# The head of a fused attention and feed-forward kernel: one written order, half of its early masks on VectorE, up weights in quarters

## The chip, the cores and the metric

The kernel runs on one core of one Trainium2 chip. The metric is device time in microseconds (us) of one execution; the median of the runs shown counts. A core has five engines that run their own instruction lists in order and meet at semaphores: TensorE (PE, with its weight loads PEld), VectorE (DVE), ScalarE (ACT), GpSimd (POOL) and SyncE (SP). POOL, SP and ACT also issue the transfers (DMAs).

## The reference

Causal attention over 8 sequences of 576 tokens with 8 heads of 64 columns and 16 extra "beacon" keys that no mask covers, and then a two-layer feed-forward with a leaky ReLU, in float32:

```python
k_all = np.concatenate([beacon_k, k], axis=2)
v_all = np.concatenate([beacon_v, v], axis=2)
scores = scale * np.matmul(q, k_all.transpose(0, 1, 3, 2))
causal[:, Nb:] = np.triu(np.ones((S, S), dtype=bool), k=1)
scores = np.where(causal, -1000000000.0, scores)
a = np.exp(scores - scores.max(-1, keepdims=True))
a /= a.sum(-1, keepdims=True) + 1e-09
x = np.matmul(a, v_all)            # then heads side by side: 4608 tokens x 512
h = x @ w_in                       # 512 x 2048
out = np.maximum(0.01 * h, h) @ w_out   # 2048 x 512
```

## The kernel before

**Units.** A unit g (0 to 31) is one pair of heads of one sequence; four units make a sequence. Keys of a unit lie in five blocks of up to 128 rows (the first holds the 16 beacons and 112 tokens). Scores are made transposed, keys on partitions and queries along the row, so a causal block needs work only on and above its diagonal.

**One unit's way.** Queries and keys are loaded as bf16 by POOL's DMAs (`load_qk`, L158) and turned by PE with an identity (`t_q`, L243), and DVE or ACT copy the result out of PSUM (L249). For unit 0 the keys come over SP in float32 (`first_k`), are cast by ACT and DVE (L928, L929) and turned at L238. `score` (L267) makes one of four groups n of score products in a PSUM tile, of which there are two, and ACT puts the exponential of it into `aT` (L276). The diagonal blocks then lose their lower triangle: `mask(g, part)` calls `triangle` (L289), a POOL affine select in place; part 0 is the first block, part 1 the blocks of groups 1 and 2, part 2 those of group 3. `value(g, half)` multiplies with the values (L359; half 0 is the first three query tiles, half 1 the last two), DVE takes the reciprocal of the row sums (L388) and multiplies (L389), and `finish` turns the result into `xT` (L405, copy at L410). Values of a sequence are loaded in five blocks (L209 the beacons, L214).

**The feed-forward.** An up step (`up`, L442) makes 128 of the 2048 hidden columns for 512 tokens in a PSUM bank, and ACT writes the leaky ReLU to `gT` (L450). A down step (`down`) multiplies `gT` with `w_out`: for the first 512 tokens four products of 512 columns each (L519), four steps making one tile of 128 tokens, and later in a scheme with seven products instead of eight (L544). `w_in` comes in two halves of 1024 columns (L131) and `w_out` in two (L137). DVE makes differences of `w_out` for that scheme (L468 to L472).

**The head and the rest.** The first two sequences (units 0 to 7) are the head; its order on every engine is the order in which the code is written, since the scheduler is told to keep it: some calls and strings that `run` reads step by step. From unit 8 on, the order follows from a list of events with due times, and there the scores are made in stretches of 512 columns (`stretch`, L314, exponentials L329 and L333) over queries and keys that DMA transposes lay out (`load_natural` L171, `turn_pair` L179). Head and rest meet in order too: the rest starts after the last step of the head. Small products with a tile of zeros (`unused`, L825; `unused_ahead`, L837) fill PE's early waits.

**The letters of `run`.** `l` load_qk, `q` and `k` turn queries or keys, `s` score, `m` mask, `v` value, `x` finish, `V` load of a value block, `u` up, `d` down, `i` and `o` loads of `w_in` and `w_out`, `N` load_natural, `T` turn_pair, `y` the transfer that turns unit 4's result, `b` the beacon columns of a later unit's keys, `t` the differences of `w_out`, `w` and `W` the products with zeros. After the letter stands the unit, then a group, half or engine: `s2.1` is group 1 of unit 2, and 1 as an engine is ACT.

**Queues.** PSUM has two score tiles and four banks that all else shares. POOL's DMAs use eight semaphores in turn: an issue waits until the transfer eight issues earlier has landed, and holds all that stands behind it on POOL, the selects too.

Of the kernel before, what the change touches and what calls it, by code (L numbers as in the profile page):

```python
# [9 lines left out]
BF16 = mybir.dt.bfloat16  # L10
AF = mybir.ActivationFunctionType
ALU = mybir.AluOpType
# [3 lines left out]
def kernel(  # L16
# [24 lines left out]
    RI = 9  # L41
# [47 lines left out]
    blank = singles.tile([128, 128], BF16, name="blank")  # L89
    w_in_sb = [singles.tile([128, NJ, DF // 2], BF16, name=f"w_in_sb{i}") for i in range(2)]  # L90
# [71 lines left out]

    def load_first_keys():
        for h in range(2):
            nc.sync.dma_start(out=first_k[h], in_=k[0, h].rearrange("(p i) d -> p i d", i=RI))
# [674 lines left out]

    NG = B * NPAIR
# [18 lines left out]
    def run(steps):  # L860
        for step in steps.split():
# [33 lines left out]
            elif op == "i":  # L895
                load_w_in(a[0])
            elif op == "o":
                load_w_out(a[0])
            elif op == "t":
                weight_sums(a[0])  # L900
            else:
                raise ValueError(step)
# [11 lines left out]
    with order:  # L914
        load_first_keys()
        load_beacon_k(0, 2, nc.scalar)
        nc.vector.memset(blank, 0.0)
        nc.vector.memset(ident, 0.0)
        run("l0.0 l1.0")
        make_identity(nc, ident, nomemset=True)  # L920
        make_ones()
        run("l1.1 l2.0 l2.1 V0.0 V0.1 l3.0 l3.1 V0.2 V0.3 V0.4 l4.0 l4.1 i0")
        make_pads()
        unused(13, 256)
        cast_beacon_k(0, 2, nc.scalar.copy)
        beacon_transposes(0, 2)
        unused(13)
        nc.scalar.copy(out=k_nat0[:, :, 0], in_=first_k[0])  # L928
        nc.vector.tensor_copy(out=k_nat0[:, :, 1], in_=first_k[1])  # L929
        run("q0.1 k0 w2.384 s0.0 m0.0 w3.256 s0.1 q1 s0.2 m0.1 k1 s0.3 m0.2")  # L930
        run("w2.384 s1.0 m1.0 q2 s1.1 k2 w2.384 s1.2 m1.1 w2.384 s1.3 m1.2 W0.0.4 s2.0 m2.0 W0.0.4 s2.1 W0.0.6 q3 l5.0 l5.1 s2.2 k3 w4.384 v0.0 m2.1 s2.3 i1 m2.2 W0.1.4 s3.0 m3.0 v1.0 s3.1 v0.1 s3.2 v1.1 m3.1 l6.0 l6.1 s3.3 x0.1 m3.2")
# [110 lines left out]
```

## Time and profile before

| | |
|---|---|
| runs | 325.3, 324.43, 329.58 us; median 325.3 us |
| profiled execution | span 323.8 us from its first to its last instruction; of its own time the profile gives no more than this span |
| PE busy | 314.3 us (97%) |
| DVE, ACT, POOL busy | 168.0, 203.8, 184.3 us |
| granted TensorE clock, mean | 1.000 |
| transfers | 39.78 MB, mean 123 GB/s |

An engine's busy share counts its own instructions; on POOL it counts the issue of DMAs, not the transfers. A timeline row holds the start, the length, the engine, the line, what is written and read, the count of merged instructions, and in brackets the idle time of the engine ahead of it with what ended it. A DMA's row is its issue; its landing shows where somebody waits for it. The chain of waits follows the program back from its last instruction.

### The profile page before, as it was taken

The page shows a single profiled execution, that of the slowest core. Times are in us where ns is not written, and L with a number is a line of the kernel's source. Part 1 is how long each engine was busy: PE and PEld are TensorE (multiplying, and loading weights), DVE is VectorE, ACT ScalarE, POOL GpSimd, SP SyncE. Part 2 cuts the span into 40 slices and gives each one's busy share as a digit, 9 for nine tenths or more (in the row PEclk, how much of TensorE's full clock was granted, in tenths as well). Part 3 has the DMA queues.
Part 4 walks back from the last instruction along what each step waited for, and adds up shares of the span by engine and source line. Part 5 has one row for each costly group of instructions (what it writes and reads, how often), then busy time and mean ns, then how long its engine had stood idle before and what let it go on. Part 6 is the DMA issues. An engine that isn't in the chain of part 4 may idle for free.

```text
span 323.8 us, 8701 instructions
## 1 busy us (share of the span) xinstructions
PE 314.3 (97%) x3468; PEld 219.1 (68%) x3494; DVE 168.0 (52%) x341; ACT 203.8 (63%) x346; POOL 184.3 (57%) x354
## 2 busy tenths in 40 slices
PE   7999999999999999999999999999999999999995
PEld 4575555444588557855788888656875697688784
DVE  3464245508255244444443454525464689577954
ACT  4968962387855786478746874687458547455510
POOL 8895868999996787659875977666221000000000
PEclk9999999999999999999999999999999999999999
DMA  8999999999999999999999999999222100200123
GB/s 137 129 189 192 124 214 140 169 177 188 135 152 160 216 138 129 114 186 97 141 176 174 99 143 119 188 128 129 44 81 82 26 2 32 75 25 2 65 67 130
DMA packets 155256, 39.78 MB, mean 123 GB/s; under 512 B 142368, under 2 KB 152480, under 8 KB 155216
## 3 DMA queue, kind: packets, MB, share of 16 engines
q0 software_dynamic: 99824, 18.54, 91.1%
q1 hardware_dynamic: 55120, 20.62, 38.3%
q8 instruction: 27, 0.44, 0.6%
q14 instruction: 13, 0.11, 0.1%
q10 hardware_dynamic: 272, 0.07, 0.1%
HBM read 37.22 MB, written 9.44 MB: 144 GB/s over the span
## 4 chain that ended last, share of the span: by engine, by line
PE 72%; DMA 14%; POOL 9%; ACT 3%; issue 1%; DVE 0%; POOLq 0%; ACTq 0%; SPq 0%
PE acc L442 24%; PE acc L544 19%; PE sc L544 11%; PE av L359 6%; PE sc L314 5%; PE acc L663 5%; DMA w_out_sb<-in_moe_w_out_dram 4%; DMA gsum<-in_k_dram 4%; POOL aT L289 3%; DMA k_nat<-in_k_dram 3%; DMA v_aug<-in_v_dram 2%; ACT aT L333 2%; DMA kT<-k_nat 2%; POOL gsum L158 1%; POOL v_aug L214 1%
## 5 line engine op out<-in xcount | busy, mean ns | idle before, releaser
L442 PE MATMUL acc<-xT,w_in_sb 128*128 128x512 bf16 (+1 forms) x537 | 116.5, 354 | 1.5 <-ACT aT L329 0.3
L450 ACT ACTIVATE gT<-acc 128x512 bf16<-128x512 f32 x124 | 70.8, 623 | 33.1 <-PE acc L442 32.6
L289 POOL TENSOR_SCALAR_AFFINE_SELECT aT<-aT 128x256 bf16<-128x256 bf16 (+2 forms) x160 | 59.7, 403 | 51.4 <-ACT aT L329 31.5
L442 PEld LDWEIGHTS <-w_in_sb 128*128 128x128 bf16 x560 | 51.7, 98 | 43.9 <-issue 2.9
L544 PEld LDWEIGHTS <-gT 128*128 128x128 bf16 x512 | 48.7, 98 | 7.7 <-issue 1.8
L333 ACT ACTIVATE aT<-sc 128x1024 bf16<-128x1024 f32 (+3 forms) x64 | 51.7, 892 | 0.0
L329 ACT ACTIVATE aT<-sc 128x512 bf16<-128x512 f32 (+3 forms) x64 | 29.0, 520 | 27.8 <-PE sc L314 27.8
L388 DVE RECIPROCAL rec<-av 128x6 f32<-128x6 f32 (+1 forms) x64 | 12.0, 187 | 65.0 <-PE av L359 64.4
L359 PEld LDWEIGHTS <-aT 128*128 128x128 bf16 (+1 forms) x960 | 36.9, 98 | 9.2 <-issue 1.4
L544 PEld LDWEIGHTS <-gsum 128*128 128x128 bf16 x384 | 36.5, 98 | 6.5 <-issue 0.4
L359 PE MATMUL av<-v_aug,aT 128*128 128x65 bf16 (+1 forms) x960 | 39.8, 194 | 0.8 <-DMA v_aug<-in_v_dram 0.4
L214 POOL DMA_DIRECT2D v_aug<-in_v_dram x40 | 34.1, 856 | 4.2 <-DMA w_in_sb<-in_moe_w_in_dram 3.8
L171 POOL DMA_DIRECT2D k_nat<-in_k_dram x48 | 34.8, 730 | 0.9 <-DMA w_out_sb<-in_moe_w_out_dram 0.3
L171 POOL DMA_DIRECT2D q_nat<-in_q_dram x48 | 34.8, 729 | 0.6 <-issue 0.4
L389 DVE TENSOR_TENSOR x_nat<-av,rec 128x384 bf16<-128x384 f32 (+1 forms) x64 | 31.4, 491 | 2.2
L544 PE MATMUL acc<-w_out_sb,gT 128*128 128x256 bf16 x240 | 28.9, 273 | 0.4 <-ACT gT L450 0.4
L276 ACT ACTIVATE aT<-sc 128x1024 bf16<-128x1024 f32 (+3 forms) x32 | 26.0, 874 | 4.7 <-PE sc L267 2.5
L314 PE MATMUL sc<-qT,kT 64*128 64x80 bf16 (+22 forms) x384 | 22.2, 250 | 0.3
L314 PEld LDWEIGHTS <-kT 64*128 64x128 bf16 x384 | 12.8, 94 | 11.2 <-issue 7.6
L544 PE MATMUL acc<-w_sum,gsum 128*128 128x256 bf16 x160 | 20.1, 273 | 0.0
L575 ACT COPY p<-acc 128x512 f32<-128x512 f32 x15 | 9.1, 604 | 16.8 <-PE acc L544 16.8
L785 DVE TENSOR_TENSOR gsum<-gT 128x1024 bf16<-128x1024 bf16 x16 | 11.0, 688 | 15.7 <-ACT gT L450 15.7
(95 smaller groups left out, 339.0 us busy)
## 6 DMA issues: line engine op xcount, KB each, us to landing
out_dram<-p SPq DMA_DIRECT2D x26, 256.0 KB, 3.2
q_nat<-in_q_dram POOLq DMA_DIRECT2D x48, 72.0 KB, 5.5
k_nat<-in_k_dram POOLq DMA_DIRECT2D x48, 72.0 KB, 5.3
v_aug<-in_v_dram POOLq DMA_DIRECT2D x24, 128.0 KB, 6.5
w_in_sb<-in_moe_w_in_dram POOLq DMA_DIRECT2D x2, 1024.0 KB, 12.4
w_out_sb<-in_moe_w_out_dram POOLq DMA_DIRECT2D x2, 1024.0 KB, 12.1
out_dram<-u SPq DMA_DIRECT2D x8, 256.0 KB, 2.7
gsum<-in_q_dram POOLq DMA_DIRECT2D x8, 144.0 KB, 7.1
```

The costliest lines, as they stand in the source:

```text
L171: nc.gpsimd.dma_start(out=t[:, :, par], in_=(q, k)[which][b, 2 * hp + par].rearrange("(t p) d -> p t d", p=NR),)
L214: nc.gpsimd.dma_start(out=dst[lo : ROWS[c], c, :, 0:D], in_=v[b, :, OFF[c] : OFF[c] + n].rearrange("h p d -> p h d"),)
L276: nc.scalar.activation(out=aT[:, :, c0 : c0 + w], in_=sc[:, :, 0:w], func=AF.Exp, scale=0.125)
L289: nc.gpsimd.affine_select(out=view, in_=view, compare_op=ALU.is_ge, fill=0.0, base=128 - n if lo == 0 else 0, channel_multiplier=-1, patte ...
L314: nc.tensor.matmul(out=(sc[par] if apart else sc[:, par])[:, at : at + b - a], lhsT=kT[ps_, c * 128 : (c + 1) * 128], rhs=qT[ps_, q0 : q0 ...
L329: nc.scalar.activation(out=probs[g][:, par, lo:hi], in_=sc[par][:, at : at + hi - lo], func=AF.Exp, scale=0.125)
L333: nc.scalar.activation(out=probs[g][:, :, lo:hi], in_=sc[:, :, at : at + hi - lo], func=AF.Exp, scale=0.125)
L359: nc.tensor.matmul(out=avv[:, n, 0 : D + 1], lhsT=aT[0 : ROWS[c], par, a0 : a0 + 128], rhs=va[0 : ROWS[c], c, 2 * hp + par, :], start=(c = ...
L389: nc.vector.tensor_tensor(out=x_nat[:, t0:t1].rearrange("p t e d -> p (t e) d"), in0=avv[:, :, 0:D], in1=rec[:, n0:n1, None].to_broadcast( ...
L442: nc.tensor.matmul(out=acc[:, lo:hi], lhsT=w_in_cols(fc, j), rhs=xT[:, j, x0 : x0 + hi - lo], start=(j == 0), stop=(j == NJ - 1), skip_gro ...
L450: nc.scalar.activation(out=gT[i][:, fc, :], in_=acc, func=AF.Prelu, alpha=0.01)
L544: nc.tensor.matmul(out=acc[:, lo : lo + HD], lhsT=left(i, n, fc, tile), rhs=right(n, fc), start=(lo == 0 and fc == 0), stop=(fc == HF - 1) ...
```

## The change

Four things are done in the head, and nothing behind it.

- A tile `kept` of ones, with zeros below its diagonal, is made once (a memset on DVE, an affine select on POOL). `mask` with a third argument multiplies the diagonal block with `kept` on VectorE, instead of the affine select on POOL. 12 of the 24 mask groups of units 0 to 7, with 20 of their 40 blocks, take this way.
- `w_in` is loaded in four pieces of 512 columns rather than in two of 1024.
- The calls between the strings get letters of their own (`F` first keys, `K`, `C`, `B` the first beacons' load, cast and turning, `h` the casts of unit 0's keys, `Z`, `I`, `J`, `j`, `O`, `P` constants, `L`, `c`, `D` the later beacons), so that all of the head is one string, `HEAD`.
- `HEAD` puts the steps in another order. The counts of score, value, transposing, up and down steps and of the products with zeros are the same as before.

```diff
+    kept = singles.tile([128, 128], BF16, name="kept")
...
-    def load_w_in(i):
-        n = DF // 2
-        loaded["w_in", i] = nc.gpsimd.dma_start(
-            out=w_in_sb[i], in_=w_in_r[:, :, i * n : (i + 1) * n]
+    def load_w_in(i, part=None):
+        lo, hi = (0, DF // 2) if part is None else (part * (DF // 4), (part + 1) * (DF // 4))
+        nc.gpsimd.dma_start(
+            out=w_in_sb[i][:, :, lo:hi], in_=w_in_r[:, :, i * (DF // 2) + lo : i * (DF // 2) + hi]
         )
...
-    def mask(g, part):
+    def mask(g, part, dve=0):
         aT = probs[g]
         for lo, n, rows in MASKS[part]:
-            triangle(aT, lo, n, rows)
+            if dve:
+                view = aT[0:rows, :, lo : lo + n]
+                at = 128 - n if lo == 0 else 0
+                nc.vector.tensor_tensor(
+                    out=view,
+                    in0=view,
+                    in1=kept[0:rows, None, at : at + n].to_broadcast([rows, 2, n]),
+                    op=ALU.mult,
+                )
+            else:
+                triangle(aT, lo, n, rows)
+
+    def make_kept():
+        nc.gpsimd.affine_select(
+            out=kept,
+            in_=kept,
+            compare_op=ALU.is_ge,
+            fill=0.0,
+            base=0,
+            channel_multiplier=-1,
+            pattern=[[1, 128]],
+        )
...
+    HEAD = "l0.0 Z I w13.256 l1.0 l1.1 w13 J F1 O w2.384 l3.0 l2.1 w3.256 l2.0 W0.0.4 K l3.1 V0.0 V0.1 q0.0 V0.2 l4.0 l4.1 F0 V0.4 w2.384 V0.3 C w2.384 h0.1 h1.0 i0.1 W0.0.6 q1 B j W0.1.4 k0.1 w2.384 P l5.0 s0.0 k1 s0.2 s0.3 i0.0 s1.0 m0.0.1 s0.1 m0.1.1 k2.1 w4.384 s1.1 q2 s1.2 W0.0.4 q3.0 s2.0 v0.0 s2.2 m1.1.1 q4.1 k3.0 s1.3 m0.2.1 m1.0.0 m1.2.0 s2.1 v1.0 s3.0 l5.1 m2.1.1 k4.0 s3.1 m2.0.0 v1.1 v0.1 l6.0 s2.3 m2.2.1 l7.1 l6.1 m3.0.1 i1.0 s3.2 m3.1 v2.0 s3.3 m3.2 V1.0 V1.2 x1.0 x0.1 v2.1 v3.0 v3.1 x2.1 q5.0 s4.0 V1.1 k5.0 x3.0 q6.1 s4.1 s4.2 u i1.1 u V1.3 m4.0.1 s5.0 k7.1 s4.3 k6.0 u l7.0 u V1.4 o0 s5.2 u u L m4.1.1 m4.2.0 v4.0 s5.1 m5.0.1 u s6.0 o1 s5.3 m5.1.1 v5.0 m6.0.0 u u s6.2 s6.1 m5.2.0 u N8.0 N8.1 v4.1 q7.0 c u v5.1 u s7.0 x5.0 m6.1.1 u y4 T8 m7.0 u s7.1 d u s7.3 s6.3 d m6.2 N9.0 s7.2 m7.1 D v6.0 v6.1 u m7.2 b8.2 v7.0 N9.1 V2.0 d N10.0 T9 v7.1 b10.2 N10.1 d T10 x6.1 b9.2 t0 d b11.2 x7.0 V2.1 d"
...
+            elif op == "F":
+                nc.sync.dma_start(out=first_k[a[0]], in_=k[0, a[0]].rearrange("(p i) d -> p i d", i=RI))
+            elif op == "h":
+                (dve, act)[a[1]](out=k_nat0[:, :, a[0]], in_=first_k[a[0]])
...
-        load_first_keys()
...
-        run("q0.1 k0 w2.384 s0.0 m0.0 w3.256 s0.1 q1 s0.2 m0.1 k1 s0.3 m0.2")
...
+        run(HEAD)
```

What this makes of three places:

VectorE, around the copies of unit 0's keys, before (tp is a PSUM tile of turned columns, k_nat unit 0's cast keys, gsum the buffer of its raw ones):

```order
L121 MEMSET aT_92 128x2x24 x2
L121 MEMSET aT_93 128x2x24 x2
L201 COPY kT<-tp 64x8x16 x2
L929 CAST k_nat_97<-gsum_96 64x9x64
L249 COPY kT<-tp 128x117
L249 COPY kT<-tp 128x459
L249 COPY qT<-tp 128x576
```

and now, from the memset of the value buffers' ones on:

```order
L126 MEMSET v_aug_90 128x40
L246 COPY qT<-tp 128x576
L942 CAST k_nat_98<-gsum_97 64x9x64
L246 COPY qT<-tp 128x576
L198 COPY kT<-tp 64x8x16 x2
L246 COPY kT<-tp 128x459
```

The queries of units 0 and 1 are copied by DVE around the cast of unit 0's keys, where before ACT copied unit 0's queries and DVE unit 1's came later; the beacon columns come after them, and the first 117 key columns go to ACT.

VectorE, from the first reciprocal (half 0 of unit 0's values) on, now (aT_91 to aT_94 are the probabilities of units 0 to 3, rec and x_nat the normalised result of a half):

```order
L406 RECIPROCAL rec<-av 128x6
L407 TENSOR_TENSOR x_nat<-av,rec 128x384
L285 TENSOR_TENSOR aT_92<-aT_92,kept 128x2x128 x2
L246 COPY kT<-tp 128x576
L285 TENSOR_TENSOR aT_91<-aT_91,kept 128x2x128
L285 TENSOR_TENSOR aT_91<-aT_91,kept 80x2x80
L406 RECIPROCAL rec<-av 128x6
L407 TENSOR_TENSOR x_nat<-av,rec 128x384
L285 TENSOR_TENSOR aT_93<-aT_93,kept 128x2x128 x2
L246 COPY kT<-tp 128x576
```

where before the halves followed each other with nothing between but the copies:

```order
L388 RECIPROCAL rec<-av 128x6
L389 TENSOR_TENSOR x_nat<-av,rec 128x384
L388 RECIPROCAL rec<-av 128x6
L389 TENSOR_TENSOR x_nat<-av,rec 128x384
L388 RECIPROCAL rec<-av 128x4
L389 TENSOR_TENSOR x_nat<-av,rec 128x256
```

Nine products with `kept` and the copies of units 3 and 4's keys and of unit 5's queries and keys now stand between that first reciprocal and the copy of unit 3's result, ahead of which no up step can begin.

POOL, behind the second half of `w_out`, before (q_nat and k_nat are loads of units 8 to 10, bk the later beacons, v_aug sequence 2's values):

```order
L188 CAST bk<-bk_raw 128x384
L171 DMA q_nat<-in_q_dram 96x6x64 x2
L289 AFFINE_SELECT aT_93<-aT_93 128x2x112
L289 AFFINE_SELECT aT_93<-aT_93 128x2x128 x3
L289 AFFINE_SELECT aT_93<-aT_93 80x2x80
L171 DMA k_nat<-in_k_dram 96x6x64 x2
L229 COPY kT<-bkT 128x16 x4
L171 DMA q_nat<-in_q_dram 96x6x64 x2
L171 DMA k_nat<-in_k_dram 96x6x64 x2
L209 DMA v_aug_88<-in_beacon_v_dram 16x8x64
```

and now:

```order
L168 DMA q_nat<-in_q_dram 96x6x64 x2
L307 AFFINE_SELECT aT_94<-aT_94 128x2x128 x3
L307 AFFINE_SELECT aT_94<-aT_94 80x2x80
L226 COPY kT<-bkT 128x16
L168 DMA k_nat<-in_k_dram 96x6x64 x2
L206 DMA v_aug_89<-in_beacon_v_dram 16x8x64
L211 DMA v_aug_89<-in_v_dram 112x8x64
L168 DMA q_nat<-in_q_dram 96x6x64 x2
L226 COPY kT<-bkT 128x16
L168 DMA k_nat<-in_k_dram 96x6x64 x2
```

The first two value loads of sequence 2 now stand ahead of unit 10's queries and keys.

More of the change, by code (lines that the diff above doesn't have):

```diff
@@ L161, in load_qk @@
         )
-    def load_first_keys():
-        for h in range(2):
-            nc.sync.dma_start(out=first_k[h], in_=k[0, h].rearrange("(p i) d -> p i d", i=RI))
     def load_natural(g, which):
@@ L895, in run @@
             elif op == "i":
-                load_w_in(a[0])
+                load_w_in(*a)
             elif op == "o":
```

47 lines of the change are left out of this document (25 added, 22 removed).

## The prediction

> **What bounds the kernel now.** I read the page first, then the chain of waits, then the timeline of the first 80 us.
>
> ```profile
> PE 314.3 (97%) x3468; PEld 219.1 (68%) x3494; DVE 168.0 (52%) x341; ACT 203.8 (63%) x346; POOL 184.3 (57%) x354
> PE   7999999999999999999999999999999999999995
> DMA  8999999999999999999999999999222100200123
> ```
>
> PE is busy in 314.3 of 323.8 us, and in the first slices too. The change leaves the number and kinds of PE's instructions as they are, so all it can win is idle time of PE: 9.5 us in the whole span, some of it before the first transfer can land. The transfers are at 9 tenths from the second slice to two thirds of the span. The chain shows where they hold the head:
>
> ```profile
> 6.09 7.05 DMA v_aug<-in_v_dram
> 22.86 11.57 DMA gsum<-in_k_dram
> 39.96 13.69 DMA w_out_sb<-in_moe_w_out_dram
> 64.21 8.28 DMA k_nat<-in_k_dram
> 72.54 5.26 DMA kT<-k_nat
> 77.85 0.67 PE sc L314 x10
> ```
>
> A value load issued at 6.09 lands at 13.14, a key load of 22.86 at 34.43, the second half of `w_out` of 39.96 at 53.65: seven, twelve, fourteen us later, since each stands behind a queue of others. So the loads of the head are one long line that runs without a break, and the time of a landing is the sum of what stands ahead of it. At 77.80 the keys of unit 11 are laid out, and PE takes them 0.05 us later. PE and the loads arrive together there; a PE that came earlier would wait.
>
> The timeline shows the few places where PE itself waits for a load or a mask (start, length, engine, line, work, idle before it):
>
> ```profile
> 5.91 0.47 PE L243 MATMUL tp<-ident,gsum 64*64 64x64 bf16 x18 [0.83 <-DMA gsum<-in_q_dram]
> 16.67 0.72 PE L359 MATMUL av<-v_aug,aT 128*128 128x65 bf16 x12
> 18.18 0.54 PE L359 MATMUL av<-v_aug,aT 128*128 128x65 bf16 x12
> 19.89 0.35 PE L359 MATMUL av<-v_aug,aT 80*128 80x65 bf16 x6 [0.39 <-DMA v_aug<-in_v_dram]
> 40.04 0.68 PE L359 MATMUL av<-v_aug,aT 128*128 128x65 bf16 x15 [0.19 <-POOL aT L289]
> 47.30 1.04 PE L519 MATMUL acc<-w_out_sb,gT 128*128 128x512 bf16 x4 [0.48 <-DMA w_out_sb<-in_moe_w_out_dram]
> 53.70 3.61 PE L519 MATMUL acc<-w_out_sb,gT 128*128 128x512 bf16 x15
> 53.94 0.72 POOL L171 DMA_DIRECT2D k_nat<-in_k_dram  x1 [0.34 <-DMA w_out_sb<-in_moe_w_out_dram]
> ```
>
> The twelve value products at 16.67 take 0.18 us longer than the same twelve at 18.18: I read that as the third value block landing at about 17.1. The third down step, at 53.70, begins when the second half of `w_out` has landed.
>
> **The change part by part.** *The start.* Rows before:
>
> ```profile
> 6.42 0.64 ACT L249 COPY qT<-tp 128x576 bf16<-128x576 bf16 x1 [1.98 <-PE tp L243]
> 5.62 0.74 DVE L929 CAST k_nat<-gsum 64x576 bf16<-64x576 f32 x1 [0.87 <-DMA gsum<-in_k_dram]
> 4.29 0.46 DVE L201 COPY kT<-tp 64x128 bf16<-64x128 bf16 x2 [2.21 <-PE tp L194]
> 7.31 0.39 PE L267 MATMUL sc<-qT,kT 64*128 64x512 bf16 x2
> 7.74 8.89 ACT L276 ACTIVATE aT<-sc 128x1024 bf16<-128x1024 f32 x11 [0.68 <-PE sc L267]
> ```
>
> The first query load still lands at about 5.9, so DVE's first copy still begins at 6.42. Then stand, one after the other on DVE, a query copy (0.76, the row further down), a cast (0.74), a second query copy (0.76) and the beacon columns (0.46): 6.42 + 2.72 = 9.14. The first score group follows at 9.2 instead of 7.31, the first exponential at 9.6 instead of 7.74. In between PE does products with zeros and a transposing that it did later before, so PE loses nothing yet; ACT is 1.9 us late. Eight exponentials of 0.81 (8.89 over 11) and one copy of 0.64 bring ACT to about 16.7, when the first value half is due. It still waits for the third value block, which has the same ten loads ahead of it as before: 17.1.
>
> *DVE from there to the first up step.* The first up step needs the copy of unit 3's result, and the order on DVE puts the following between the first reciprocal (17.43 before, and now) and the end of that copy. Means by form (busy us, mean ns):
>
> ```profile
> L249 DVE COPY qT<-tp 128x576 bf16<-128x576 bf16 x7 | 5.3, 756 | 12.7 <-PE tp L243 12.7
> L389 DVE TENSOR_TENSOR x_nat<-av,rec 128x384 bf16<-128x384 f32 x32 | 17.8, 557 | 1.1
> L389 DVE TENSOR_TENSOR x_nat<-av,rec 128x256 bf16<-128x256 f32 x32 | 13.6, 424 | 1.1
> L388 DVE RECIPROCAL rec<-av 128x6 f32<-128x6 f32 x32 | 6.2, 194 | 35.8 <-PE av L359 35.5
> L388 DVE RECIPROCAL rec<-av 128x4 f32<-128x4 f32 x32 | 5.8, 180 | 29.2 <-PE av L359 28.9
> L410 DVE COPY xT<-tp 128x576 bf16<-128x576 bf16 x6 | 2.7, 455 | 5.2 <-PE tp L405 5.2
> L785 DVE TENSOR_TENSOR gsum<-gsum,gT 128x1024 bf16<-128x1024 bf16 x16 | 11.0, 690 | 0.4
> L469 DVE TENSOR_TENSOR w_sum<-w_out_sb,w_sum 128x2048 bf16<-128x2048 bf16 x1 | 1.2, 1225 | 0.0
> 26.07 1.90 PE L442 MATMUL acc<-xT,w_in_sb 128*128 128x512 bf16 x7
> ```
>
> A product with `kept` has no row. From 1024 to 2048 elements a product of two bf16 tiles grows by 0.535 us; taken down to 256 elements that is 0.690 - 0.75 x 0.535 = 0.29 us, which I take. Its bounds are 0.18 (the short reciprocal) and 0.42 (256 elements read from PSUM). Four first halves are 4 x 0.751 = 3.0, four second halves 4 x 0.604 = 2.4, four key and query copies 3.0, two result copies 0.9, nine products 2.6: 11.9 us, and 17.43 + 11.9 = 29.4 for the first up step, against 26.07 (28.4 to 30.6 by the product's bounds). Before, those halves had no products and three fewer copies among them. Here DVE takes the end from PE.
>
> Some of this is only moved: by then PE has also turned three more tiles and made one more score group:
>
> ```profile
> 28.30 0.75 PE L243 MATMUL tp<-ident,gsum 64*64 64x64 bf16 x36
> 27.90 0.48 PE L267 MATMUL sc<-qT,kT 64*128 64x336 bf16 x8
> 20.45 0.73 PE L359 MATMUL av<-v_aug,aT 128*128 128x65 bf16 x18
> 25.68 0.43 PE L405 MATMUL tp<-ident,x_nat 112*128 112x112 bf16 x5
> ```
>
> That is 1.5 x 0.75 + 0.24 = 1.4 us, so PE is 3.3 - 1.4 = 1.9 us behind.
>
> *From there to the third down step.* Before, 53.70 - 26.07 = 27.6 us. Of these 1.4 are already done; a value half (0.73) and the turning of unit 6's result (0.43) have gone behind the third down step, 1.2; and the waits of 0.19 and 0.48, with 0.2 ahead of 53.70, close when PE comes two us later. 27.6 - 1.4 - 1.2 - 0.9 = 24.1, and 29.4 + 24.1 = 53.5. The loads ahead of the second half of `w_out` are the same set as before, so it lands at 53.65 again: PE has caught up, and waits. What went behind that point comes on top: **1.2 us**. I take 1.1, as a short wait for unit 8's keys at 61 can absorb a little.
>
> *`w_in` in quarters.* Two more issues, same bytes, and a piece of 2 KB rows where there were 4 KB ones. Landings show no price for a further load in a full line:
>
> ```profile
> 26.30 0.90 POOL L214 DMA_DIRECT2D v_aug<-in_v_dram  x1 [0.84 <-DMA w_in_sb<-in_moe_w_in_dram]
> 32.23 0.73 POOL L214 DMA_DIRECT2D v_aug<-in_v_dram  x1 [2.92 <-DMA w_in_sb<-in_moe_w_in_dram]
> ```
>
> The halves land just ahead of 26.30 and 32.23; between the second and the key load of 34.43 two loads land, 1.2 us each with all they carry. So two more cost 0 at best and 2 x 1.2 = 2.4 us at worst if their bytes were free; I take 0. The Trainium skill, DMA: Bandwidth & Descriptors, in its section on the anatomy of one DMA, gives each DMA about 2.0 us beside its bytes; paid in line, two more would be 4 us and the sum 330.4. Loads that land 1.2 us apart say that this part overlaps.
>
> *The masks that leave POOL.* POOL loses 20 selects, about 8 us by the row below, but its issues wait for landings in that stretch (0.84 and 2.92 above), so the loads go no faster: worth 0 here, save for the wait of 0.19 counted above.
>
> **The rivals.** *The waits go and nothing replaces them.* If DVE finds gaps for its products, PE keeps its pace and loses the waits of 0.39, 0.19, 0.48 and about 0.2 and 0.2, 1.5 us, and up to 1 us more at the start. For it: POOL's masks do stand behind load issues that wait for landings (2.92 at 32.23). Against it: unit 11's keys at 77.80. It gives 324.3, or 322.8 at best.
>
> *Unit 9's to 11's loads come late.* On POOL the last masks of unit 7 now stand ahead of unit 9's keys, and two value loads ahead of unit 10. From 53.94 POOL issues without a break to 64.21, so each us put in there reaches 77.80: about 0.8 of masks and, for unit 10, 1.4 of value issues. PE then waits up to 2 us beyond the 1.1: 328.
>
> *VectorE and GpSimd block each other.* This ends slower:
>
> ```profile
> 74.31 2.30 DVE L472 TENSOR_TENSOR w_out_sb<-w_out_sb 128x2048 bf16<-128x2048 bf16 x1
> 74.78 2.79 POOL L289 TENSOR_SCALAR_AFFINE_SELECT aT<-aT 128x256 bf16<-128x256 bf16 x5
> L289 POOL TENSOR_SCALAR_AFFINE_SELECT aT<-aT 128x256 bf16<-128x256 bf16 x24 | 9.2, 410 | 1.1 <-ACT aT L276 0.9
> ```
>
> Side by side, a product that takes 1.225 alone takes 2.30, and five selects take 2.79 instead of about 2.0. The products with `kept` are of this kind, and run beside the other half of the selects. If each of the 20 waits out a select of 0.41 on the path, that is 8.2 us on top of 1.1: 334.6. It ends over 2% slower from about 0.27 us per product. The Trainium skill, SBUF — State Buffer, section "Who interferes with whom", states that a VectorE instruction with two SBUF inputs contends with a GpSimd one that reads SBUF; the trace agrees, by the 2.30 against 1.225. But 20 selects fill only 8 of the 40 us from 14 to 54, and the second half of `w_out` hides the first 0.2 us and what DVE has spare behind it.
>
> **How the numbers follow.** The sum is on the profiled span, 323.8 + 1.1 = 324.9; the median lies 1.5 above that span, so I forecast 325.3 + 1.1 = **326.4 us**. Chances: the forecast's case (324.8 to 327.6) 0.50, the waits that go 0.27, the late loads 0.17, the blocking 0.06. The range takes in the best of the second and the third with the product's upper bound (1.2): 322.8 to 329.6. Two per cent, 6.5 us, is about what a measurement of this kernel can tell from no change; only blocking passes it upwards, and a gain of that size would need two thirds of all PE's idle time: faster 0.02, same 0.92, slower 0.06.
>
> **What would show it.** The first exponential at about 9.6; a product with `kept` at 0.29; DVE without idle time from 17.4 to the first up step at about 29.4; the second half of `w_out` landing at 53.7 with PE waiting for it; the first stretch of scores at 62.3; unit 11's keys at about 78. I am wrong if the third value block lands well ahead of 17 (then ACT and DVE start their chain earlier), if DVE idles in that stretch, or if the second half of `w_out` lands more than 1 us off 53.65.

## The result and the profile after

| | before | after |
|---|---|---|
| median of 20 executions each, one chip | 325.21 us | 326.65 us |
| ratio | | 1.0055, 95% interval 1.0028 to 1.0081 |
| lowest, highest | 323.18, 330.52 | 325.43, 331.08 |
| profiled execution: its time, its span | 325.3, 323.8 | 325.43, 323.7 |

Forecast were 326.4 us, 322.8 to 329.6, and no change that a measurement can tell: both hold. The way to them, as the experiments show, was largely another. (A ratio leaves out executions that lie more than 1.5% above the fastest of their kernel, here three of before and four of after.)

A warning stands ahead of the reading: the profiled execution of after is the fastest of its twenty, and its span is that of before. So this trace shows what the new order does when nothing goes wrong. From its page (busy time, then busy tenths and the transfers' share in 40 slices):

```profile
PE 314.2 (97%) x3469; PEld 219.9 (68%) x3494; DVE 170.1 (53%) x358; ACT 205.3 (63%) x350; POOL 180.0 (56%) x337
PE   8899999999999999999999999999999999999995
DMA  8999999999999999999999999999222100200123
```

POOL's busy time is 4.3 us shorter and DVE's 2.1 us longer; PE's is where it was. The timeline of the head after:

```profile
8.69 0.42 PE L235 MATMUL tp<-ident,k_nat 64*128 64x64 bf16 x9 [0.32 <-DVE qT L246]
9.48 0.39 PE L264 MATMUL sc<-qT,kT 64*128 64x512 bf16 x2
9.92 4.12 ACT L273 ACTIVATE aT<-sc 128x1024 bf16<-128x1024 f32 x5 [0.52 <-PE sc L264]
10.99 0.30 PE L264 MATMUL sc<-qT,kT 64*128 64x208 bf16 x4 [0.43 <-ACT aT L273]
11.75 0.39 PE L264 MATMUL sc<-qT,kT 64*128 64x512 bf16 x2 [0.45 <-ACT aT L273]
13.91 0.68 DVE L285 TENSOR_TENSOR aT<-aT,kept 128x224 bf16<-128x224 bf16 x3 [2.56 <-POOL kept L295]
16.37 0.20 DVE L406 RECIPROCAL rec<-av 128x6 f32<-128x6 f32 x1
27.16 0.45 DVE L428 COPY xT<-tp 128x576 bf16<-128x576 bf16 x1
27.81 1.47 PE L460 MATMUL acc<-xT,w_in_sb 128*128 128x512 bf16 x5
30.82 0.74 POOL L211 DMA_DIRECT2D v_aug<-in_v_dram  x1 [0.90 <-DMA w_in_sb<-in_moe_w_in_dram]
34.13 0.76 POOL L138 DMA_DIRECT2D w_out_sb<-in_moe_w_out_dram  x1
49.17 0.81 PE L537 MATMUL acc<-w_out_sb,gT 128*128 128x512 bf16 x3 [0.16 <-issue]
52.99 0.65 PE L377 MATMUL av<-v_aug,aT 128*128 128x65 bf16 x9 [0.29 <-POOL aT L307]
53.48 1.03 PE L537 MATMUL acc<-w_out_sb,gT 128*128 128x512 bf16 x4
61.56 0.85 PE L332 MATMUL sc<-qT,kT 64*128 64x512 bf16 x12
77.62 0.83 PE L332 MATMUL sc<-qT,kT 64*128 64x96 bf16 x16
```

The first score stands at 9.48 and the first exponential at 9.92, two microseconds later than before, and PE then waits for a score tile twice within a microsecond (10.99, 11.75). From there the order makes good what it lost: the first up step comes at 27.81 (26.07 before), the third down step at 53.48 (53.70), the first stretch of scores at 61.56 (61.15), unit 11's stretch at 77.62 (77.85). POOL issues the second half of `w_out` at 34.13, 5.8 us earlier than before (39.96), and it lands at 49.18 by the landing records, 4.5 us earlier; PE waits for it no more. The products with `kept`, by form:

```profile
L285 DVE TENSOR_TENSOR aT<-aT,kept 128x256 bf16<-128x256 bf16 x14 | 3.7, 297 | 0.7 <-ACT aT L273 0.5
L285 DVE TENSOR_TENSOR aT<-aT,kept 128x224 bf16<-128x224 bf16 x4 | 1.1, 268 | 2.6 <-POOL kept L295 2.6
L285 DVE TENSOR_TENSOR aT<-aT,kept 80x160 bf16<-80x160 bf16 x2 | 0.5, 230 | 0.0
```

The chain of waits leaves the loads for PE at unit 10's keys now, where it did at unit 11's before:

```profile
59.76 4.42 DMA k_nat<-in_k_dram
64.23 7.33 DMA kT<-k_nat
71.61 0.72 PE sc L332 x10
```

Unit 11's stretch does not wait for its keys any more. Nothing in this trace accounts for the 1.4 us between the medians. That was the question for the experiments.

### The profile page after: what moved, and what is told of

The parts are those of the page before. It is cut to its first block, busy times and chain, and to the rows that moved or that the text cites. A ratio compares the mean times of both kernels' runs of the same rounds, so it can differ in the third digit from the quotient of the medians.

```text
span 323.7 us, 8695 instructions
## 1 busy us (share of the span) xinstructions
PE 314.2 (97%) x3469; PEld 219.9 (68%) x3494; DVE 170.1 (53%) x358; ACT 205.3 (63%) x350; POOL 180.0 (56%) x337
## 4 chain that ended last, share of the span: by engine, by line
PE 84%; ACT 6%; DMA 5%; POOL 2%; issue 1%; DVE 0%; ACTq 0%; SPq 0%; POOLq 0%
PE acc L460 29%; PE acc L562 19%; PE sc L562 11%; PE av L377 9%; PE sc L332 6%; PE acc L681 5%; ACT aT L273 3%; DMA kT<-k_nat 2%; PE sc L264 2%; ACT aT L351 2%; DMA gsum<-in_q_dram 1%; DMA k_nat<-in_k_dram 1%; PE acc L537 1%; PE tp L240 1%; POOL q_nat L168 1%
## 5 line engine op out<-in xcount | busy, mean ns | idle before, releaser
L307 POOL TENSOR_SCALAR_AFFINE_SELECT aT<-aT 128x256 bf16<-128x256 bf16 (+2 forms) x140 | 52.8, 406 | 61.1 <-ACT aT L347 30.9
L406 DVE RECIPROCAL rec<-av 128x6 f32<-128x6 f32 (+1 forms) x64 | 11.9, 187 | 65.2 <-PE av L377 64.4
```

Source lines behind the costliest of these rows:

```text
L307: nc.gpsimd.affine_select(out=view, in_=view, compare_op=ALU.is_ge, fill=0.0, base=128 - n if lo == 0 else 0, channel_multiplier=-1, patte ...
```

## The experiments

The kernels fall into four sets. Each set ran on one chip, beside the kernel before on the same chip, and the four sets had four chips. The changed kernel itself ran in the first and third set only, so in the second and fourth a kernel can be compared with the kernel before, and with the changed kernel only across chips. Every execution has its mean granted clock of PE (the share of the full clock that it was given), and this turned out to carry most of the story.

**First set: which part costs.** The kernel before had a median of 325.12 us here (17 executions).

*The changed kernel again*, nothing edited.

> The changed kernel once more, to see a second profile of it. In the first profile its span is 323.7 us against 323.8 before, while the median of its runs is 0.55% above. Theory 1 (a fixed loss in the order of the head): the ratio is again about 1.005, and a second profile shows a head that ends 1 to 2 us later than in the first. Theory 2 (the loads land at other times from run to run, and the new order leans on them more): the third value block (16.0 us in the first profile) and the second half of w_out (49.2) land a microsecond or more elsewhere, and the span moves with them.

Measured: 330.70 us (6 executions, 327.97 to 331.59), ratio 1.0161 (1.0127 to 1.0194). On this chip the change costs three times as much, so theory 1's 1.005 is not repeated. Four of the six executions have a mean clock of 0.979, which no execution of the kernel before has there (all 0.998 or more). The profiled one (0.994) shows a stall, and what follows it. First the timeline of PE, then the table by stretches (start and end, length, busy time of PE, PEld, DVE, ACT, POOL, granted clock, transfers' share, GB/s):

```profile
27.68 0.47 PE L240 MATMUL tp<-ident,gsum 64*64 64x64 bf16 x18
30.76 0.55 PE L264 MATMUL sc<-qT,kT 64*128 64x464 bf16 x6 [2.61 <-issue]
77.73 0.72 PE L332 MATMUL sc<-qT,kT 64*128 64x256 bf16 x10 [1.47 <-DMA kT<-k_nat]
```

```profile
25.27:28.69 3.42, 2.88 (x90) 2.29 (x86) 3.32 (x10) 2.17 (x3) 3.42 (x6) 1.00 1.22 192
28.69:32.10 3.41, 1.34 (x10) 0.62 (x11) 0.19 (x2) 1.07 (x3) 2.95 (x5) 1.00 2.83 141
32.10:35.51 3.41, 3.41 (x31) 1.27 (x31) 0.00 (x0) 2.69 (x5) 1.39 (x2) 0.50 1.62 191
```

PE stands still for 2.6 us and waits for nothing that the profile shows ("issue"); in the next 3.41 us it is granted half its clock. Later PE waits 1.47 us for unit 10's keys: POOL issues their loads from 63.94 on, against 59.04 in the trace of after, which the chain of waits leads back to PE's own delay, and the transfer that lays the keys out then takes 8.36 us where it took 7.33. Up to the second half of `w_out` the landings lie within 0.7 us of those in the trace of after, so late loads (theory 2) are not the cause.

*The new order without the products.*

```diff
-            elif op == "I": ... nc.vector.memset(kept, 1.0)
-HEAD = "... B j W0.1.4 ... m0.0.1 s0.1 m0.1.1 ... m6.1.1 ..."
+HEAD = "... B W0.1.4 ... m0.0 s0.1 m0.1 ... m6.1 ..."
```

> The new order and the quarters, with all 40 mask blocks as affine selects on POOL. If the products on VectorE cost the time (they stand between copies that PE waits for), this is at the time of before, ratio 1.000. If the order alone costs it, the ratio stays at 1.004 to 1.008. If the products are what makes the new order possible (POOL's selects then wait behind load issues and hold PE, and the loads behind them issue late), it is slower than the changed kernel: 1.010 or more.

Measured: 332.87 us (6 executions, 327.34 to 334.14), with no ratio: one execution alone stays within 1.5% of the fastest. The median is 2.2 us above the changed kernel's. At a clock of 0.979 its two executions (332.53, 333.63) lie above the changed kernel's four (329.82 to 331.59), but the one execution of each with the full clock says the opposite (327.34 here, 327.97 there). So the times don't show whether the products on VectorE are a gain in the new order. The profile, of the execution with the full clock, shows what they avoid: PE waits twice for masks on POOL, and the first up step comes at 29.60.

```profile
24.55 0.27 PE L377 MATMUL av<-v_aug,aT 128*128 128x65 bf16 x3 [0.84 <-POOL aT L307]
25.66 1.38 PE L377 MATMUL av<-v_aug,aT 128*128 128x65 bf16 x27 [0.85 <-POOL aT L307]
```

That the products cost the time (ratio 1.000 without them) is excluded: all six executions are above the kernel before's median.

*The new order with `w_in` in halves.*

```diff
-HEAD = "... h1.0 i0.1 ... s0.3 i0.0 s1.0 ... l6.1 m3.0.1 i1.0 ... u i1.1 u ..."
+HEAD = "... h1.0 i0 ... s0.3 s1.0 ... l6.1 m3.0.1 i1 ... u u ..."
```

> The changed kernel with w_in in two halves, each at the place of its first quarter. If two more loads in the line cost what two landings cost there (0.6 to 1.2 us each), this is 1 to 2 us faster than the changed kernel, ratio to before about 1.000; the forecast took that price at 0, so that the ratio stays at 1.004 to 1.008.

Measured: 330.68 us (328.61 to 332.76), ratio 1.0168 (1.0129 to 1.0207): as the changed kernel, 330.70. Quarters or halves make no difference to the median that these six executions can tell. With halves POOL's issue of `w_out` waits 4.08 us for a half of `w_in`, the transfer eight issues earlier, and a value block of the second sequence comes late for PE:

```profile
36.78 0.77 POOL L138 DMA_DIRECT2D w_out_sb<-in_moe_w_out_dram  x1 [4.08 <-DMA w_in_sb<-in_moe_w_in_dram]
40.75 0.44 PE L377 MATMUL av<-v_aug,aT 128*128 128x65 bf16 x9 [2.35 <-DMA v_aug<-in_v_dram]
```

The second half of `w_out` lands at 54.43 here, at 48.73 in the changed kernel's trace on this chip, and at 50.33 with quarters and all masks on POOL. These are single profiles, and what PE's clock does moves the landing too: in the changed kernel's trace of the third set, with half clock until 26.85, it lands at 53.11. The nearest pair is this trace and that of the emptied start of the second set, with quarters and half clock for the same stretch (until 22.01 and 21.80): 54.43 against 49.57. So the quarters probably bring the landing forward by some 5 us; for the masks that leave POOL no share is shown.

*The order of before with the products.* The same 12 mask groups, `kept` made behind the identity:

```diff
-run("q0.1 k0 w2.384 s0.0 m0.0 w3.256 s0.1 q1 s0.2 m0.1 k1 s0.3 m0.2")
+run("q0.1 k0 w2.384 s0.0 m0.0.1 w3.256 s0.1 q1 s0.2 m0.1.1 k1 s0.3 m0.2.1")
```

> The order and the halves of before, with the same 12 mask groups as products on VectorE, and the kept triangle made behind the identity. If the products take nothing from the path and end the waits of PE for masks (0.19 and, by their order, some behind 14.2), the ratio is 0.997 to 1.000. If VectorE's 20 products of 0.25 us push the copies that PE waits for, it is 1.003 to 1.008, and the loss of the change is theirs.

Measured: 326.59 us (12 executions), ratio 1.0051 (1.0018 to 1.0084). In the old order the products cost half a per cent. The trace shows how: a product that waits for its exponential stands on VectorE ahead of the copy of unit 1's keys, PE waits for that copy, and in the next 3.41 us the clock is halved. Three executions with the full clock, at 329.31 to 330.18, show that something else has a part in this median.

```profile
10.39 0.29 DVE L289 TENSOR_TENSOR aT<-aT,kept 128x256 bf16<-128x256 bf16 x1 [0.38 <-ACT aT L277]
11.41 0.39 PE L268 MATMUL sc<-qT,kT 64*128 64x512 bf16 x2 [1.02 <-DVE kT L250]
```

**Second set: the clock.** Theory A was formed on the traces of the first set: PE is granted half its clock for one or more windows of 3.41 us after a window in which it was little used. The window's place against the program differs in each execution. The kernel before had 325.39 us on this chip (35 executions).

*The start filled.* 14 products with zeros of 384 columns at six places (the text below counts seven) where the changed kernel's PE waits between 10 and 19 us:

```diff
-HEAD = "... s0.2 s0.3 i0.0 s1.0 m0.0.1 s0.1 ... W0.0.4 q3.0 s2.0 v0.0 s2.2 ..."
+HEAD = "... s0.2 G3 s0.3 i0.0 G3 s1.0 m0.0.1 G2 s0.1 ... W0.0.4 G2 q3.0 G2 s2.0 v0.0 G2 s2.2 ..."
+            elif op == "G":   # a[0] products of 384 columns of zeros into the bank of value half (0, 1)
```

> The changed kernel with 14 more products with zeros (384 columns, 0.16 us each) on TensorE, at the seven places between 10 and 19 us where its trace shows TensorE waiting for a score tile or a query load. Theory A (clock): the changed kernel is slow where TensorE is busy for less than half of one clock window of 3.41 us and the granted clock is halved for the following 1 to 4 windows; the start's windows stand at 45 to 56%. Filled, they stand at 75% or more: median 326 to 327.5 us on this chip and a mean granted clock of 0.995 or more in most executions, though TensorE has 2.2 us more to do. Theory B (the order itself costs 1 to 1.6%, whatever the clock): 330 to 333 us, and a clock as in the changed kernel.

Measured: 327.04 us (12 executions, 326.06 to 328.41), ratio 1.0053 (1.0028 to 1.0078). All twelve have a clock of 0.998 or more. With the waits filled the clock no longer falls; but the time is not back at the kernel before.

*The start emptied.* Four of the last five groups of products with zeros left out (`W0.1.4` stays):

```diff
-HEAD = "... i0.1 W0.0.6 q1 B j W0.1.4 k0.1 w2.384 P ... k2.1 w4.384 s1.1 q2 s1.2 W0.0.4 q3.0 ..."
+HEAD = "... i0.1 q1 B j W0.1.4 k0.1 P ... k2.1 s1.1 q2 s1.2 q3.0 ..."
```

> The changed kernel without its last five groups of products with zeros (those after the casts of unit 0's keys: 6 of 112 columns, 2 of 384, 4 of 384, 4 of 112), 1.4 us of TensorE work that lies in waits. Theory A (clock): more windows below half, so the clock is halved in nearly every execution (mean 0.98 or lower): 331 to 334 us. Theory B: this work costs nothing and its absence brings nothing: 330 to 331, as the changed kernel on this chip.

Four groups are listed and left out, not five. Measured: 327.16 us (12 executions, 326.07 to 328.33), ratio 1.0063 (1.0036 to 1.0090). All twelve executions have a mean clock of 0.978 to 0.990, so the clock falls in each. The time, though, is that of the filled start: theory A's price, 331 to 334, is wrong here. (Filling adds some 2 us of work to PE and emptying takes some away, so the two times do not isolate the clock's price.) The profile's stretches, first the empty one and then the next:

```profile
8.14:11.56 3.42, 1.79 (x37) 1.16 (x37) 2.66 (x14) 2.05 (x4) 2.69 (x5) 1.00 1.91 159
11.56:14.97 3.41, 3.37 (x48) 1.68 (x49) 1.11 (x4) 3.25 (x5) 3.41 (x6) 0.50 2.16 141
```

*The old order emptied*: all products with zeros from the first score group on left out of the kernel before.

```diff
-run("q0.1 k0 w2.384 s0.0 m0.0 w3.256 s0.1 q1 ...")
-run("w2.384 s1.0 m1.0 q2 s1.1 k2 w2.384 s1.2 ... W0.0.4 s2.0 m2.0 W0.0.4 s2.1 W0.0.6 q3 ... w4.384 v0.0 ... W0.1.4 s3.0 ...")
+run("q0.1 k0 s0.0 m0.0 s0.1 q1 ...")
+run("s1.0 m1.0 q2 s1.1 k2 s1.2 ... s2.0 m2.0 s2.1 q3 ... v0.0 ... s3.0 ...")
```

> The kernel before without its products with zeros from the first score group on (14 of 384 columns or pairs of them, 3 of 256, 18 of 112; about 3.5 us of TensorE work in waits). Theory A (clock): the old order goes the same way once its windows stand below half: mean clock 0.98, 328 to 331 us. Theory B: 325 us as before, with a clock of 1.0.

The edit leaves out 12 products of 384 columns, not 14. Measured: 325.60 us (12 executions), ratio 1.0022 (0.9994 to 1.0051). Eleven of twelve now have a clock of 0.977 to 0.984: the old order loses its clock too once it is emptied. And it costs at most half a per cent, against theory A's 328 to 331. In both emptied kernels the half clock of the profiled execution ends by 20.02 and 21.80, and the first up step is hardly later for it (26.32 against 26.07 before, 28.92 against 28.74 in the filled start): it lay, it seems, in time in which PE would have waited.

*The old start of unit 0.* The first query copy on ScalarE, the second behind the first score group:

```diff
-HEAD = "... V0.1 q0.0 V0.2 ... W0.0.6 q1 B j W0.1.4 k0.1 w2.384 P l5.0 s0.0 k1 s0.2 ..."
+HEAD = "... V0.1 q0.1 V0.2 ... W0.0.6 B j W0.1.4 k0 w2.384 P l5.0 s0.0 q1 k1 s0.2 ..."
```

> The changed kernel with unit 0's first query copy on ScalarE and its second behind the first score group, as in the kernel before, so that the first score comes 1.5 us earlier. If the late start is what costs (it moves all that follows and lowers the windows at 8 to 15 us): 326.5 to 328 us and clock drops in fewer executions. If what comes after the start costs: 330 to 331 us, as the changed kernel.

Measured: 326.03 us (12 executions), ratio 1.0035 (1.0009 to 1.0062). The first score stands at 8.77 instead of 9.48, which is 0.7 us earlier and not 1.5. Ten of twelve executions have 0.997 or more and the other two 0.994. This is the smallest edit, and with it nearly all clock drops are gone. The time is below the range that either case gave; since the changed kernel was not beside it, how much of that is the edit and how much the chip stays open.

**Third set: the fetch of instructions.** Theory C: the stall without a wait in the first set's trace is the fetch of PE's own instructions. It stands ahead of PE's 956th instruction, and in three traces there is one at this very place: 2.77 us in the first set, 0.91 with the old start, 0.29 in the profile of after (from the last product's start, less its columns' time; the timeline's own figures, by modelled ends, are a little less). Two rows of the trace of the first set, for 28.1 to 29.2, and one of the old start's timeline:

```profile
q0 software_dynamic: 570, 0.18, 151.0%
q8 instruction: 1, 0.02, 5.3%
```

```profile
27.52 0.55 PE L264 MATMUL sc<-qT,kT 64*128 64x464 bf16 x6 [0.75 <-issue]
```

By the packets' records such a block of 16 KB lands at 29.12, 26.15 and 25.97 in the three, and PE goes on 1.64, 1.37 and 1.35 us later. The Trainium skill, Runtime: NRT & Kernel Launch, section on instruction fetch mechanics, says that instructions come in 16 KB blocks of 256 and that crossing a block's edge is mostly hidden; 27 packets with 0.44 MB on this queue agree, the 2.77 us do not.

The kernel before had 324.93 us on this chip (25 executions). *The changed kernel, a third time*:

> The changed kernel once more, as the control on this chip. Theory C (instruction fetch): TensorE's own instructions come in blocks of 16 KB over a queue of their own; the third block that the trace shows lands at 26 to 29 us behind the loads, and TensorE stands still without any wait ahead of its 956th instruction, the second part of group 1 of unit 4, until 1.4 to 1.6 us after that landing: 0.3 to 2.8 us, different in each execution. So the time is 326 to 331 us, wider than that of the kernel before. Theory B (a fixed loss in the order): a narrow spread round one value, with no stall there.

Measured: 328.34 us (8 executions, 325.07 to 332.17), ratio 1.0097 (1.0065 to 1.0129). Seven of eight executions have a clock under 0.995. The profile, by stretches:

```profile
6.37:9.78 3.41, 3.09 (x69) 2.39 (x67) 2.49 (x5) 0.00 (x0) 3.37 (x5) 1.00 1.36 181
9.78:13.20 3.42, 2.38 (x39) 1.18 (x35) 1.95 (x12) 2.73 (x5) 1.80 (x3) 1.00 1.81 142
13.20:16.61 3.41, 3.41 (x44) 1.64 (x42) 0.69 (x3) 2.60 (x4) 3.22 (x6) 0.50 1.47 119
23.44:26.85 3.41, 3.41 (x56) 2.57 (x52) 2.29 (x7) 1.81 (x3) 3.30 (x6) 0.50 0.84 112
26.85:30.26 3.41, 3.41 (x91) 3.06 (x89) 2.91 (x12) 2.35 (x5) 1.96 (x5) 1.00 1.02 138
```

This is the case that the timed executions with 0.979 point to (four windows of 3.41 us at half clock are 4 x 3.41 x 0.5 / 324 = 2.1%). The window from 9.78 to 13.20 holds PE's waits for score tiles, which the next rows show, and the clock is halved from 13.20 to 26.85:

```profile
11.80 0.30 PE L264 MATMUL sc<-qT,kT 64*128 64x208 bf16 x4 [0.43 <-ACT aT L273]
12.56 0.39 PE L264 MATMUL sc<-qT,kT 64*128 64x512 bf16 x2 [0.45 <-ACT aT L273]
32.49 1.69 PE L460 MATMUL acc<-xT,w_in_sb 128*128 128x512 bf16 x6
```

The first up step comes at 32.49 instead of 27.81. There is no stall at the 956th instruction, since PE comes there late. So neither theory C's stall in each execution nor theory B's narrow spread is what came.

*Fewer instructions*: the products with zeros of the changed kernel merged into wider ones, the same columns in 60 instructions fewer.

```diff
-HEAD = "l0.0 Z I w13.256 l1.0 l1.1 w13 J ... w3.256 l2.0 ... w4.384 s1.1 ..."
+HEAD = "l0.0 Z I w6.512 w1.256 l1.0 l1.1 w3.512 w1 J ... w2.384 l2.0 ... w3.512 s1.1 ..."
-        for i in range(n):   # unused_ahead: n products of 112 columns
+        for r in (3, 3) if n == 6 else (n,):   # products of r x 112 columns
...
```

> The changed kernel with its products with zeros merged into wider ones: the same number of columns, 60 instructions fewer on TensorE, all ahead of 20 us, and nothing else moved. Theory C: the boundary of the block then lies 60 instructions further on, in the up steps, which TensorE reaches about 3 us later (its 1016th instruction of before stood at 30.1 us), while the block is asked for only 1 us later: no stall without a wait at 25 to 31 us, a narrower spread, and 0.5 us (where the changed kernel's fetch was quick) to 3 us faster than the changed kernel on this chip. Theory B: the same time as the changed kernel.

Measured: 327.20 us (12 executions), ratio 1.0073 (1.0036 to 1.0110). No stall without a wait is in its trace. Its times fall into steps by the clock: five executions at 0.998 or more, 325.39 to 326.20 (four of them within 0.07 us of each other); three at 0.984 to 0.989, 327.18 to 328.41; four at 0.979, 329.82 to 330.22. So on one chip and in one kernel four half-clock windows go with 4.5 us, two or three with 2 to 3. The 1.1 us to the changed kernel are within the intervals of both, and the executions with the full clock are no faster than the changed kernel's one (325.07), so this run does not show that the fetch costs anything on average.

*The same merging in the kernel before*:

> The kernel before with the same merging of its products with zeros. Theory C: before, TensorE reaches its 956th instruction at 29.0 us, and the block had landed at 27.4, so it lost nothing or a few tenths: within 0.5 us of the kernel before, faster if anything. Theory B: the same time as the kernel before.

Measured: 325.58 us (12 executions), ratio 1.0024 (0.9998 to 1.0051): no gain.

**Fourth set: both remedies together.** The old start, the merged products, and two products of 384 columns ahead of unit 1's first score group (`G2 s1.0`).

> The changed kernel with three things together: unit 0's query copies in the places of the kernel before, the products with zeros merged (60 instructions fewer on TensorE), and two more products of 384 columns ahead of unit 1's first score group. Theory A (clock: a window of 3.41 us in which TensorE is busy for under 49% halves the next ones) and theory C (instruction fetch) together: no window of the first 30 us under 55%, a mean granted clock of 0.998 or more in all executions, no stall without a wait at 26 to 31 us, and 325.0 to 325.8 us, within 0.3% of the kernel before on the same chip. If the new order loses something else as well: a clock of 1.0 and still 0.4% or more above the kernel before.

Measured: 325.46 us (12 executions, 324.77 to 327.64) beside 324.99 for the kernel before (17 executions), ratio 1.0029 (1.0009 to 1.0050). All twelve have a clock of 0.997 or more, and its trace has no stall without a wait at 26 to 31 us. One window goes down to 50% by the measure below, where no window under 55% was expected:

```profile
14.47:17.89 3.42, 2.39 (x71) 1.50 (x66) 2.85 (x7) 3.30 (x6) 0.77 (x2) 1.00 3.23 120
```

So the drops are gone, and what the new order loses besides is 0.3%. The profile does not show where: its first stretch of scores, at 60.91, comes ahead of that of the kernel before, 61.15. No kernel of the study beats the kernel before.

**The clock, over all traces.** PE's use of a window is estimated from the starts of its matmuls: its columns at 2.4 per ns (256 columns start 0.11 us apart at full clock) or half of that at half clock, and only gaps of over 0.06 us count as idle. This gives less than the busy time of the views, whose ends are modelled. Windows are those that the granted clock's own edges give, from the clock's first record on. That record comes at 3.8 to 7.1 us, in one trace at 10.46. Ahead of it the products are at half pace in every trace (256 columns 0.213 us apart, 0.11 behind it), though the mean clock does not count this. In two traces of the new order in which it comes late, the first score is late too: 10.30 and 10.57 with records at 6.37 and 7.06, against 9.48 with 3.82.

| kernel | least window | half clock | first up step | first stretch | executions under 0.997 |
|---|---|---|---|---|---|
| before | 53% | none | 26.07 | 61.15 | 1 of 94 |
| changed, profile of after | 51% | none | 27.81 | 61.56 | 11 of 20 |
| changed, first set | 37% at 28.69 | 32.10 to 35.51 | 31.24 | 66.45 | 5 of 6 |
| changed, third set | 44% at 9.78 | 13.20 to 26.85 | 32.49 | 66.25 | 7 of 8 |
| fewer instructions | 43% at 10.48 | 13.89 to 27.54 | 32.61 | 66.44 | 7 of 12 |
| new order without products | 52% | none | 29.60 | 63.64 | 5 of 6 |
| halves | 48% at 8.36 | 11.77 to 22.01 | 30.48 | 67.37 | 4 of 6 |
| old order with products | 46% at 9.31 | 12.73 to 16.14 | 27.51 | 61.79 | 7 of 12 |
| start emptied | 32% at 8.14 | 11.56 to 21.80 | 28.92 | 62.67 | 12 of 12 |
| old order emptied | 47% at 6.37 | 9.78 to 20.02 | 26.32 | 61.11 | 11 of 12 |
| old order, fewer instructions | 66% | none | 26.68 | 60.42 | 2 of 12 |
| start filled | 61% | none | 28.74 | 62.49 | 0 of 12 |
| old start | 56% | none | 28.00 | 61.76 | 2 of 12 |
| both remedies | 50% | none | 27.16 | 60.91 | 0 of 12 |

Every full-clock window of 48% or less that this table names is followed by half clock; after one of 50% or more the full clock stays. One window outside it speaks against a plain threshold: 42%, from 39.08 in the kernel with halves, had no consequence. From the first up step to the first stretch it is 33.75 us in the profile of after, 33.76 and 33.83 with four windows at half clock: in these traces what is lost ahead of the first up step is lost for good. The share that the clock has in each execution is not all: two executions of the halves with 0.998 and 1.000 took 328.61 and 329.29 us, and one of after with 1.000 took 328.73.

## Why the prediction was right, and where it was not

- **Start: right.** First score 9.2 and first exponential 9.6 were forecast, 9.48 and 9.92 came. What I did not ask is what the late start does to PE's use: by the prediction's own words "PE loses nothing yet". With the waits at 8.69, 10.99 and 11.75 a window can have as little as 42% (the thinnest 3.41 us at the start of the profile of after, from 8.25, by the measure of the last table); the thinnest between 7 and 20 us before has 57%. The clock falls in 23 of 34 executions, and in 2 of 12 with the earlier first score. The clock was neither a term of the sum nor a rival. This is the step that failed.
- **Third value block at 17.1: wrong.** It landed at 16.00, and the first value half stood at 15.79. That it has "the same ten loads ahead of it as before" is true, but the line of loads ran faster: the block landed between 15.06 and 16.00 in all ten traces of the new order, and between 14.62 and 17.07 in the four of the old. Why is not shown.
- **The product with `kept`, 0.29 us: right**, 0.297. **DVE without idle time: nearly right**, it is busy in 10.47 of the 11.24 us from the first reciprocal to the end of unit 3's copy, and takes the end from PE as forecast. **First up step at 29.4: wrong.** It came at 27.81. I had added all of DVE's work from 17.43 on in a row. It began a microsecond earlier (the first reciprocal at 16.37), and 16.37 + 11.9 gives 28.3; the rest are pieces that the trace shows nearer than by their means, 0.24 us from one product to the next.
- **24.1 us from there to the third down step: 25.7.** The sum took 1.4 us of PE's work as already done and closed the small waits. A wait of 0.29 for a mask stands again at 52.99; how the rest of the 1.6 us divides is not shown. The two errors, 1.6 early and 1.6 long, cancel by luck, and the third down step came at 53.48 where 53.65 was forecast.
- **The second half of `w_out` at 53.65 with PE waiting: wrong.** It was issued at 34.13 instead of 39.96 and landed at 49.18. The term that failed is the landing worked out from "the same set as before": the set is the same, but with `w_in` in quarters POOL waits less for the transfer eight issues back (0.90 us at 30.82 where it was 2.92 at 32.23). It was a gain in the loads that PE could not use, since its own work ended no earlier. PE did not wait there, so the 1.1 us for what "went behind that point" are not the loss that was measured. First stretch: 61.56 against 62.3.
- **Quarters and masks worth 0: right for the time**, as far as 330.68 against 330.70 can tell, and wrong for the loads, as just said. A price of 4 us in line is excluded by these two medians, whose intervals are 1.1 and 1.3 us to each side.
- **The rivals.** The waits went in part, as the first rival had it, and were replaced by others. The late loads of units 9 to 11 were seen once (1.47 us for unit 10's keys at 77.73), where PE was already 4.9 us late. VectorE and GpSimd did not block each other: in the profile of after 19 of the 20 products took 0.23 to 0.29 us and one 0.45, and the selects of 256 elements that stayed on POOL took 0.420 us on the mean up to 62 us, against 0.410 before.
- **The number.** 326.65 lies beside 326.4 because the median of the first chip falls among executions with the full clock or close to it, about 1 us above the kernel before (nine with 0.997 or more, median 326.25), and the seven with 0.977 to 0.979, which is four half-clock windows (median 330.55), lie above it. On another chip the same kernel's median was 330.70, above the range. That the number held is luck: it depends on which executions fell to the median, and the wait for `w_out` from which the forecast took its 1.1 us did not occur.

**What stays open.** Why the new order loses 0.3% at the full clock with both remedies, and how much the remedies gain beside the changed kernel on one chip; whether the fetch of instructions costs anything on average, since the place was reached in time in the kernels that were to show it; why the clock falls for one window in some executions and for four in others; and why nine of the 94 executions of the kernel before in the four sets, and some of the others, lie 4 to 5 us higher with a clock of 0.999 or more.

## What to carry to other kernels

A reorder that leaves PE's work the same can still change its clock: count how much PE does in each 3.41 us, wherever the window may lie, and keep it over half wherever the time behind it is PE's. Products with zeros in a wait did it here, and so did an earlier first score. Half clock until 20 to 22 us cost little in the emptied kernels, where PE would have waited; until 26.85 or 27.54, close to the first up steps, it went with 4.5 us. So ask when it ends. And look at the mean granted clock of every execution before reading one profile: the profiled one may be the one to which nothing happened.

## What the runs showed of the hardware

- PE's granted clock is halved for 1 to 4 windows of 3.41 us after a window with 32 to 48% of use. In five of the seven cases no single gap is longer than 0.65 us (the rows of the third set are one of them); in the other two there is one of 1.2 and one of 2.8 us. The Trainium skill, TensorE: Matmul & The Clock Gate, Part 1, states a free-running window of 3413 ns, and the edges here agree; in its section "Why this matters for your kernels" it asks, against drops in mid-kernel, for no idle gaps of over about 3 us, and these runs show that this is not enough.
- Once halved, the clock came back after windows in which the half-speed PE was in use for 75 to 92%, and stayed half after others of 62 to 86%; what decides it is not seen.
- Ahead of the first record of the granted clock PE's products run at half pace (256 columns in 0.213 us, against 0.11 behind it), until 3.8 to 7.1 us after the start and once until 10.46.
- PE can stand still for up to 2.77 us with no semaphore to wait for, at the same instruction in three executions, and go on 1.35 to 1.64 us after a 16 KB block of its instructions has landed. The loads were dense at the time (the transfers' share is 2.83 in the stretch above, 1.22 in the one before). That the block is the cause is argued from these times and the place, not shown by a run.
